# Batch 1's complex product by three real products instead of four, with its sums, and three minima, moved to GpSimd

## The chip, the cores and the metric

One core of a Trainium2 chip runs the whole program. Its engines are TensorE (PE, with PEld for its weight loads), VectorE (DVE), ScalarE (ACT), GpSimd (POOL) and SyncE (SP, which only issues DMAs here). Each engine works through its own queue in order and waits on semaphores for the others. The metric is the device time of one execution in microseconds (us); lower is better.

## The reference, cut to what matters

```python
def _attn_ref(x, w_r, w_i, b_r, b_i):            # x: 8 batches x 3008 x 256
    X = np.fft.rfft(x, axis=1)
    Xr, Xi = X.real, X.imag
    Yr = Xr @ w_r - Xi @ w_i + b_r
    Yi = Xr @ w_i + Xi @ w_r + b_i
    lam = 0.01                                    # soft threshold of both parts
    Yr = np.sign(Yr) * np.maximum(np.abs(Yr) - lam, 0.0)
    Yi = np.sign(Yi) * np.maximum(np.abs(Yi) - lam, 0.0)
    return np.fft.irfft(Yr + 1j * Yi, n=x.shape[1], axis=1)

def _moe_ref(x, w_in, w_out):                     # 24064 x 256, 256 x 2048, 2048 x 256
    h = x @ w_in
    g = np.where(h > 0.0, h, np.exp(np.minimum(h, 0.0)) - 1.0)
    return g @ w_out
```

The output of the first part, its 8 batches one after the other, is the input of the second.

## The kernel before, in words

The second part is the bulk of the work and sets the beat. It runs in steps `i = 0 .. 375`, 47 for a batch (`PER`). A step makes one piece of the hidden layer: `front(i)` multiplies `w_in` by the transposed batch `yT` into two banks of PSUM, `hps` (four matmuls of 512 columns, line 1118; four banks in all, so step i+2 writes the banks of step i); ACT takes the exponential into `Et`; somebody takes the minimum with 1 (`elu`: POOL at line 1169 when the step is "pooled", DVE at line 1171 otherwise; in a step that is "on_act" ACT makes it by another route, lines 1128 and 1133); DVE joins `Et` and `hps` into `gT` (lines 1159 and 1161); and two steps later (`LAG`) `back(i)` multiplies `gT` by `w_out` into `ps_o` (eight matmuls, line 1192). Every eighth step closes a block of 512 rows: DVE and ACT copy `ps_o` to `osb` (line 1203), which SP sends out; the next block writes the same two banks.

Between the steps lies the first part, for the batch after. It is cut into units, and `plan(b)` writes down by hand which unit of batch b+1 goes into which step while batch b's hidden layer runs:

- A, X: the forward transform. A puts its result through DRAM into `Z`. X unit u makes an eighth of the spectrum `XT` from Z and has ACT copy it out of PSUM. In batch 1 units 2g and 2g+1 together use up quarter g of Z; a quarter is 8 neighbours out of every 32 columns of XT.
- M: the complex product, twelve groups of 128 frequencies, two for each of six `Y` tiles. DVE adds the bias into `yb`, POOL clips (`clip`) and subtracts, which is the soft threshold, and `turn_Y` sends the finished Y tile by DMA to `Yx`.
- B, Y: the inverse transform. B unit v needs `Yx` v; its result goes through DRAM to `Bs`, from which Y units make `yT`.

In the order of the code a step's units `f0` come first, then `front(i)`, then DVE's `gT` of step i-1, then the step's `f1` (stores, loads, `turn_Y`), then the minimum of step i, then `back(i-2)`. That is the order on each engine's queue.

Batch 0's first part runs before step 0. While batch 0's hidden layer runs (`plan(0)`), batch 1 gets: X units 0 to 7 in steps 10 to 17, M groups 0 to 5 in steps 18 to 23, B unit 0 in step 24, M groups 6 and 7 in 25 and 26, B 1 in 27, M in 28 and 29, B 2 in 30, M in 31 and 32, B 3 to 5 in 33 to 35, and A units of batch 2 from step 36. The x of batch 2 is loaded on POOL's queue in steps 12, 15 and 18, behind a `gate` in step 12 that waits for Z. A step with an M group is on_act; in plan(0) the other steps from 10 on have their minimum on DVE unless they are free of units.

There are two ways of the complex product. Batches 0 and 1 (`m_group`, line 292) use four products, each of 512 columns with real and imaginary outputs side by side: Xr by (w_r, w_i) and Xi by (-w_i, w_r). From batch 2 on (`unit_M` below its first branch, line 334) there are three of 256 columns: k1 = (Xr + Xi) w_r, then Xi by -(w_r + w_i) and Xr by (w_i - w_r), which with k1 give the two parts. Each is two matmuls, over the halves (`dt`) of the 256 channels. For that POOL adds Xr + Xi (`sum_XT` into the six chunks of `XS` and `busy`, line 260); `three_weights` replaces the weights and one bias by their differences on POOL (lines 276 and 279) in steps 47 to 50; DVE makes two additions from PSUM (lines 340 and 341); POOL adds a bias (line 346), clips (349) and subtracts (350). `XS` lies where `M3` was, of which a copy, `M3x`, is sent in step 6. In PSUM the M groups of batch 1 now share one pair of banks per Y tile ("psF", as the X and B units have it); the later batches have two single banks, `ps` and `k1` ("psM").

Of the kernel before, what the change touches and what calls it, by code (L numbers as in the profile page):

```python
# [24 lines left out]
NS = 32  # L25
# [4 lines left out]
def kernel(  # L30
# [224 lines left out]
    def sum_XT(b, dt, chunks=range(3)):  # L255

        XT = XT_of[b]
        for ch in chunks:
# [3 lines left out]
            )  # L262

    def sum_of(dt, ch):

        if 3 * dt + ch == 5:
            return busy[:]
        if not XS_of:
            XS_of.append(sump.tile([P, 5, 512], BF16, name="XS", tag="XS"))
        return XS_of[0][:, 3 * dt + ch]  # L270

    def three_weights(c, dt):
# [4 lines left out]
        if c == dt == 0:  # L277
            b_r_, b_i_ = (bias_bc[:, D * k : D * k + D] for k in range(2))
            nc.gpsimd.tensor_tensor(b_i_, b_i_, b_r_, ALU.subtract)

    mps_of = {}

# [26 lines left out]
    def unit_M(b, q, i):  # L309
        if b == 1:  # L310
            if i == 0:
                mps_of[q] = unit_ps("mps", False)
            yb, clip = m_group(b, q, i, mps_of[q][:, i, :])
            nc.gpsimd.tensor_scalar(clip[:], yb, LAM, -LAM, ALU.min, ALU.max)
            nc.gpsimd.tensor_tensor(Y_of[b, q][:, i, :], yb, clip[:], ALU.subtract)
            return
        XT, o = XT_of[b], (2 * q + i) * P
# [11 lines left out]
        ]  # L329
        if o == 0 and b > 3:  # L330
            todo.append(todo.pop(0))
# [17 lines left out]
        nc.gpsimd.tensor_scalar(clip[:], yb[:], LAM, -LAM, ALU.min, ALU.max)  # L349
        nc.gpsimd.tensor_tensor(Y_of[b, q][:, i, :], yb[:], clip[:], ALU.subtract)  # L350

# [870 lines left out]
    def plan(b):  # L1222
# [38 lines left out]
        for t, u in enumerate(seq, lead):  # L1261
# [19 lines left out]
            else:  # L1281
                f0[t].append(put(u[0], n1, *u[1:]))
            if u[0] == "M" and u[2] == 1:
                f1[t].append((turn_Y, (n1, u[1])))
            if u == ("B", 5):
# [18 lines left out]
        if n2 < B:  # L1304
            for ci in range(3):
                f1[xs[ci]].append((load_x, (n2, ci)))
        if b and n1 < B:
            f0[seq.index(("X", 4))].append((sum_XT, (n1, 0)))
            f0[seq.index(("X", 7))].append((sum_XT, (n1, 1, range(2 if b < 3 else 3))))
            if b < 3:  # L1310
                f0[seq.index(("M", 2, 0))].insert(0, (sum_XT, (n1, 1, (2,))))
# [5 lines left out]
    for i in range(n + LAG):  # L1317
# [6 lines left out]
        elif i < n:  # L1324
# [12 lines left out]
            else:  # L1337
                on_act = any(f is unit_M for f, a in f0[r])
                pooled = free or i < FILL
            third = calm and bare % 3 == (2 if i // PER == B - 1 else 1)  # L1340
            h = front(i, third, on_act)
        finish_elu()
        if i < n:
# [5 lines left out]
            elu(i, *h, pooled, on_act)  # L1349
            if PER <= i < PER + 4:  # L1350
                three_weights(*divmod(i - PER, 2))
            if 1 <= i < 5:
# [41 lines left out]
```

## Time and profile before

| | us |
|---|---|
| median of 3 runs (lowest, highest) | 871.36 (871.35, 871.52) |
| the profiled execution | 871.1 |
| its span, first to last instruction | 869.3 |
| PE busy | 860.8 |
| ACT busy | 715.4 |
| DVE busy | 666.2 |
| POOL busy | 592.8 |

Busy times are sums over the whole span; matmuls are pipelined, so PE's contains overlaps. In a line of the timeline stand the start, the time from the first start to the last end of the instructions merged in it, the engine, the line of the kernel, the operation, what it writes and reads, the shape, how many instructions (x), and in brackets how long the engine had been idle and who ended that. In a line of groups stand the count (x), the busy time in us, the mean of one in ns and the idle time before.

### The profile page before, as it was taken

The numbers are of one execution on the slowest core, as the hardware profiler recorded it, in microseconds if no ns is written. First come the engines' busy times: TensorE is split into PE (matmuls) and PEld (weight loads), VectorE is DVE, ScalarE is ACT, GpSimd is POOL, SyncE is SP. The second block draws the span as 40 slices with busy tenths as digits, with TensorE's granted clock in tenths as the row PEclk, the third lists the DMA queues.
The fourth block names the chain that finished last, engine by engine and source line by source line (L and its number), as shares of the span: only waits on it lengthen the run. The fifth ranks groups of instructions, "written<-read, shape, count | busy, mean of one in ns | idle before, by whom it ended". The sixth has DMA issues, their size and how long they took to land.

```text
span 869.3 us, 18553 instructions
## 1 busy us (share of the span) xinstructions
PE 860.8 (99%) x6773; PEld 675.8 (78%) x6773; DVE 666.2 (77%) x1103; ACT 715.4 (82%) x1255; POOL 592.8 (68%) x866
## 2 busy tenths in 40 slices
PE   8999999999999999999999999999999999999997
PEld 6567677887788877887778877787877888787776
DVE  8889779697676886778866787677777687788775
ACT  8878888888978889798887988879887888876664
POOL 8671651898657986588846987459874697734664
PEclk9999999999999999999999999999999999999999
DMA  8897446532575135653365432753337313250111
GB/s 248 282 288 213 117 131 193 164 117 73 141 224 170 51 79 168 191 170 92 89 183 172 128 104 78 217 165 107 94 96 213 90 39 85 79 141 25 40 36 49
DMA packets 113597, 116.11 MB, mean 134 GB/s; under 512 B 11569, under 2 KB 103473, under 8 KB 110145
## 3 DMA queue, kind: packets, MB, share of 16 engines
q1 hardware_dynamic: 108512, 86.74, 35.2%
q0 software_dynamic: 4704, 27.92, 9.8%
q8 instruction: 53, 0.87, 0.4%
q14 instruction: 40, 0.32, 0.1%
q10 hardware_dynamic: 288, 0.26, 0.1%
HBM read 53.28 MB, written 48.23 MB: 117 GB/s over the span
## 4 chain that ended last, share of the span: by engine, by line
PE 94%; POOL 2%; DVE 1%; DMA 1%; ACT 1%; issue 0%; DVEq 0%; POOLq 0%
PE ps_o L1192 39%; PE hps L1118 34%; PE mps L334 5%; PE xps L242 3%; PE mps L1118 2%; PE yps L615 2%; PE bps L451 2%; PE mps L292 2%; PE aps L194 2%; POOL Y L350 1%; DMA xt<-in_x_dram 1%; PE aps L186 0%; POOL yb L346 0%; POOL clip L349 0%; DVE gT L1159 0%
## 5 line engine op out<-in xcount | busy, mean ns | idle before, releaser
L1159 DVE SCALAR_TENSOR_TENSOR gT<-Et,hps 128x512 fp32r<-128x512 f32 x630 | 403.1, 682 | 137.0 <-POOL Et L1169 127.0
L1192 PE MATMUL ps_o<-w_out_r,gT 128*128 128x256 f32 x3008 | 477.2, 301 | 0.0
L1192 PEld LDWEIGHTS ps_o<-w_out_r,gT 128*128 128x128 f32 x3008 | 404.4, 189 | 48.0 <-DVE osb L1203 0.2
L1169 POOL TENSOR_SCALAR Et<-Et 128x512 f32<-128x512 f32 x482 | 287.3, 615 | 203.1 <-ACT Et L1130 201.6
L1118 PE MATMUL hps<-yT,w_in_s 128*128 128x512 bf16 (+7 forms) x1620 | 366.7, 353 | 0.3
L1130 ACT ACTIVATE Et<-hps 128x512 f32<-128x512 f32 x514 | 282.7, 610 | 41.7 <-PE hps L1118 38.6
L1118 PEld LDWEIGHTS <-w_in_s 128*128 128x128 bf16 x1728 | 144.1, 98 | 104.7 <-issue 13.1
L1128 ACT ACTIVATE Et<-hps 128x512 f32<-128x512 f32 x192 | 104.5, 597 | 42.0 <-PE hps L1118 41.6
L1133 ACT ACTIVATE Et<-Et 128x512 f32<-128x512 f32 x192 | 110.5, 632 | 0.0
L350 POOL TENSOR_TENSOR Y<-yb,clip 128x512 bf16<-128x512 f32 x72 | 92.7, 1287 | 6.0
L346 POOL TENSOR_TENSOR yb<-yb,bias_bc 128x256 f32<-128x256 f32 x72 | 53.2, 738 | 11.3 <-DVE yb L341 11.2
L150 ACT CAST XT<-xps 128x768 bf16<-128x768 f32 x57 | 45.8, 804 | 14.1 <-PE xps L242 13.9
L341 DVE TENSOR_TENSOR yb<-mps,yb 128x512 f32<-128x512 f32 x72 | 49.8, 692 | 7.2
L150 ACT CAST yT<-yps 128x752 bf16<-128x752 f32 x56 | 44.1, 787 | 13.7 <-PE yps L615 13.5
L1161 DVE SCALAR_TENSOR_TENSOR gT<-hps,Et 128x512 fp32r<-128x512 f32 x78 | 50.2, 686 | 3.3
L349 POOL TENSOR_SCALAR clip<-yb 128x512 f32<-128x512 f32 x72 | 44.1, 613 | 6.3
L150 ACT CAST A<-aps 128x1024 bf16<-128x1024 f32 x40 | 40.7, 1018 | 8.1 <-PE aps L194 5.0
L150 ACT CAST Bz<-bps 128x1024 bf16<-128x1024 f32 x41 | 41.6, 1014 | 5.3 <-PE bps L451 5.0
L340 DVE TENSOR_TENSOR yb<-mps,bias_bc 128x256 f32<-128x256 f32 x72 | 30.5, 424 | 17.5 <-PE mps L334 15.7
L334 PE MATMUL mps<-wcat_s,XT 128*128 128x256 bf16 x288 | 43.2, 273 | 0.0
L1203 DVE COPY osb<-ps_o 128x512 f32<-128x512 f32 x46 | 31.7, 690 | 5.4 <-PE ps_o L1192 3.4
L260 POOL TENSOR_TENSOR XS<-XT 128x512 bf16<-128x512 bf16 x30 | 34.1, 1157 | 2.4 <-ACT XT L150 1.4
(216 smaller groups left out, 673.3 us busy)
## 6 DMA issues: line engine op xcount, KB each, us to landing
xt<-in_x_dram POOLq DMA_DIRECT2D x21, 1024.0 KB, 5.3
out_dram<-osb SPq DMA_DIRECT2D x154, 128.0 KB
Bs<-DB SPq DMA_DIRECT2D x30, 384.0 KB
Yx<-Y SPq DMA_DIRECT2D x166, 64.0 KB
DA<-A SPq DMA_DIRECT2D x19, 512.0 KB
DB<-Bz SPq DMA_DIRECT2D x19, 512.0 KB
Z<-DA SPq DMA_DIRECT2D x21, 384.0 KB
xt<-in_x_dram POOLq DMA_DIRECT2D x6, 512.0 KB, 6.2
```

The source lines that it names most:

```text
L150: nc.scalar.copy(dst, src)
L334: nc.tensor.matmul(out_, lhsT=lhs[:, dt] if lhs is not None else sum_of(dt, ch)[:, oc : oc + P], rhs=w[:, dt, :], start=(dt == 0), stop=(d ...
L346: nc.gpsimd.tensor_tensor(yb[:, D : 2 * D], yb[:, D : 2 * D], bias_bc[:, D : 2 * D], ALU.add)
L350: nc.gpsimd.tensor_tensor(Y_of[b, q][:, i, :], yb[:], clip[:], ALU.subtract)
L1118: nc.tensor.matmul(hps[s][:, c0:c1], lhsT=w_in_s[:, dt, ft * P : ft * P + P], rhs=yT_of[b][:, dt, t0 : t0 + c1 - c0], start=(dt == 0), sto ...
L1128: nc.scalar.activation(Et[:, s], hps[s], AF.Relu, scale=-1.0)
L1130: nc.scalar.activation(Et[:, s], hps[s], AF.Exp)
L1133: nc.scalar.activation(Et[:, s], Et[:, s], AF.Exp, scale=-1.0)
L1159: nc.vector.scalar_tensor_tensor(o, e, -1.0, h, ALU.add, ALU.max)
L1161: nc.vector.scalar_tensor_tensor(o, h, 0.0, e, ALU.max, ALU.add)
L1169: nc.gpsimd.tensor_scalar(e, e, 1.0, 0.0, ALU.min, ALU.max)
L1192: nc.tensor.matmul(po[q][:, j, :], lhsT=gT[:, s, i_ * P : i_ * P + P], rhs=w_out_r[:, ft, :], start=(ft == 0 and j == 0), stop=(ft == NFT ...
```

## The change

Batch 1's M groups take the second way, three products. Its sums are not made by `sum_XT` but by a new `sum_part`, once for each quarter of Z, behind the X units 1, 3, 5 and 7 (steps 11, 13, 15 and 17): three additions on POOL over rows of 8 neighbours, for chunks 0 to 2, 3 to 4 and 5. As in the batches above 3, the product with the sum comes last in batch 1's very first group. `three_weights` moves from steps 47 to 50 to steps 10 to 13. The last subtraction of the batch, of group 11 in step 32, goes from POOL to DVE (`finish_Y`), behind DVE's `gT` of step 31 and ahead of the DMAs of that Y tile. In the steps of B units 0, 1 and 2 of plan(0) (24, 27 and 30) the minimum is POOL's instead of DVE's.

```diff
+    def sum_part(b, g):
+        XT, k = XT_of[b], slice(8 * g, 8 * g + 8)
+        def by_m(v):
+            return v.rearrange("p (m s) -> p m s", s=NS)[:, :, k]
+        sum_of(0, 0)
+        XS, m = XS_of[0][:], 2 * 512
+        for out_, dt, m0, m1 in (
+            (XS[:, 0:3].rearrange("p c n -> p (c n)"), 0, 0, 3 * 512),
+            (XS[:, 3:5].rearrange("p c n -> p (c n)"), 1, 0, m),
+            (busy[:], 1, m, 3 * 512),
+        ):
+            nc.gpsimd.tensor_tensor(
+                by_m(out_), by_m(XT[:, dt, 0, m0:m1]), by_m(XT[:, dt, 1, m0:m1]), ALU.add
+            )
...
     def unit_M(b, q, i):
-        if b == 1:
-            if i == 0:
-                mps_of[q] = unit_ps("mps", False)
-            yb, clip = m_group(b, q, i, mps_of[q][:, i, :])
-            nc.gpsimd.tensor_scalar(clip[:], yb, LAM, -LAM, ALU.min, ALU.max)
-            nc.gpsimd.tensor_tensor(Y_of[b, q][:, i, :], yb, clip[:], ALU.subtract)
-            return
...
-        if o == 0 and b > 3:
+        if o == 0 and (b == 1 or b > 3):
             todo.append(todo.pop(0))
...
-        nc.gpsimd.tensor_tensor(Y_of[b, q][:, i, :], yb[:], clip[:], ALU.subtract)
+        if (b, q, i) == (1, 5, 1):
+            late_Y.append((Y_of[b, q][:, i, :], yb, clip))
+        else:
+            nc.gpsimd.tensor_tensor(Y_of[b, q][:, i, :], yb[:], clip[:], ALU.subtract)
+
+    late_Y = []
+
+    def finish_Y():
+        Y, yb, clip = late_Y.pop()
+        nc.vector.tensor_tensor(Y, yb[:], clip[:], ALU.subtract)
...
             if u[0] == "M" and u[2] == 1:
+                if (b, u[1]) == (0, 5):
+                    f1[t].append((finish_Y, ()))
                 f1[t].append((turn_Y, (n1, u[1])))
...
-        if b and n1 < B:
+        if b == 0:
+            for g in range(4):
+                f0[lead + 2 * g + 1].append((sum_part, (n1, g)))
+        elif n1 < B:
...
-                pooled = free or i < FILL
+                pooled = free or i < FILL or any(f is unit_B and a[1] < 3 for f, a in f0[r])
...
-            if PER <= i < PER + 4:
-                three_weights(*divmod(i - PER, 2))
+            if FILL <= i < FILL + 4:
+                three_weights(*divmod(i - FILL, 2))
```

More of the change, by code (lines that the diff above doesn't have):

```diff
@@ L279, in three_weights @@
             nc.gpsimd.tensor_tensor(b_i_, b_i_, b_r_, ALU.subtract)
-    mps_of = {}
     def m_group(b, q, i, ps, biased=False):
```

## The prediction

> **What bounds the kernel now.** I read the page first, its shares of busy time and its chain of waits:
>
> ```profile
> span 869.3 us, 18553 instructions
> PE 860.8 (99%) x6773; PEld 675.8 (78%) x6773; DVE 666.2 (77%) x1103; ACT 715.4 (82%) x1255; POOL 592.8 (68%) x866
> ...
> PE 94%; POOL 2%; DVE 1%; DMA 1%; ACT 1%; issue 0%; DVEq 0%; POOLq 0%
> ```
>
> TensorE (PE) carries 94% of the chain. Time taken off its instruction stream is time gained, as long as no other engine becomes late at that place. The timeline then shows one M step of batch 1 (steps 18 to 32; four products of 512 columns, line 292) and one of batch 2, which already has the form that batch 1 is to get (six of 256, line 334):
>
> ```profile
> 86.31 0.61 PE L292 MATMUL mps<-wcat_r,XT 128*128 128x512 bf16 x2
> ...
> 87.18 1.03 PE L1118 MATMUL hps<-yT,w_in_s 128*128 128x512 bf16 x4
> ...
> 88.97 0.61 PE L292 MATMUL mps<-wcat_r,XT 128*128 128x512 bf16 x2
> ...
> 179.33 0.39 PE L334 MATMUL mps<-wcat_r,XS 128*128 128x256 bf16 x2
> ...
> 179.76 0.42 DVE L340 TENSOR_TENSOR yb<-mps,bias_bc 128x256 f32<-128x256 f32 x1
> ...
> 180.00 1.03 PE L1118 MATMUL hps<-yT,w_in_s 128*128 128x512 bf16 x4
> ...
> 180.29 0.69 DVE L341 TENSOR_TENSOR yb<-mps,yb 128x512 f32<-128x512 f32 x1
> ...
> 180.90 1.27 DVE L1159 SCALAR_TENSOR_TENSOR gT<-Et,hps 128x512 fp32r<-128x512 f32 x2
> ...
> 181.79 0.39 PE L334 MATMUL mps<-wcat_r,XS 128*128 128x256 bf16 x2
> ```
>
> PE goes from one M group to the hidden layer in 0.87 us with four products, in 0.67 us with six, and from one M step to the next in 2.66 and 2.46 us. So the change is worth 12 x 0.20 = 2.4 us on PE, 0.28% of the time. That is also the most it can give. 0.2% (1.7 us) is about what a measurement of this kernel can tell from no change.
>
> **What GpSimd (POOL) must do for it.** The first row here is the batch's first M group today; the others are batch 2's, where POOL has the work that batch 1 is to get:
>
> ```profile
> 85.68 0.61 POOL L314 TENSOR_SCALAR clip<-yb 128x512 f32<-128x512 f32 x1 [13.28 <-DVE yb L302]
> ...
> 176.86 0.39 PE L334 MATMUL mps<-wcat_r,XS 128*128 128x256 bf16 x2
> ...
> 178.59 0.75 POOL L346 TENSOR_TENSOR yb<-yb,bias_bc 128x256 f32<-128x256 f32 x1 [0.39 <-DVE yb L341]
> ...
> 181.36 0.74 POOL L346 TENSOR_TENSOR yb<-yb,bias_bc 128x256 f32<-128x256 f32 x1
> ...
> 182.18 0.61 POOL L349 TENSOR_SCALAR clip<-yb 128x512 f32<-128x512 f32 x1
> ...
> 182.88 1.29 POOL L350 TENSOR_TENSOR Y<-yb,clip 128x512 bf16<-128x512 f32 x1
> ...
> 184.13 0.74 POOL L346 TENSOR_TENSOR yb<-yb,bias_bc 128x256 f32<-128x256 f32 x1
> ```
>
> Before batch 1's M groups POOL sat idle for 13.28 us. With the new form it needs 184.13 - 181.36 = 2.77 us for each M group, and PE brings one every 2.46. Batch 2 has at most four M groups in a row; batch 1 has six (steps 18 to 23) ahead of its first B step. There POOL falls behind by 0.31 us a group, and the change puts one more thing into its queue at that very place, the minimum of B steps 0 to 2.
>
> **The sums.** For each quarter of Z: 384, 256 and 128 elements.
>
> ```profile
> L260 POOL TENSOR_TENSOR XS<-XT 128x512 bf16<-128x512 bf16 x30 | 34.1, 1157 | 2.4 <-ACT XT L150 1.4 <-DVE XT L148 1.0
> ...
> L971 POOL TENSOR_SCALAR w_in_s<-w_in_f 128x256 bf16<-128x256 f32 x4 | 4.7, 1170 | 0.3
> ...
> L276 POOL TENSOR_TENSOR wcat_s<-wcat_r,wcat_s 128x256 bf16<-128x256 bf16 x2 | 1.3, 672 | 0.0
> ```
>
> Lines 260 and 276 (512 and 256 elements in 1157 and 672 ns) give 1.9 ns an element and 0.19 us an instruction: 0.92 + 0.67 + 0.43 = 2.0 us a quarter, if rows of eight neighbours, 64 bytes apart, run like whole rows. That is the low end. The high end is line 971, which reads single elements 16 bytes apart: (1170 - 190) / 256 = 3.8 ns, so 3.5 us a quarter. I take the low end, since within a row of eight the step is that of line 260. The Trainium skill (GPSIMD Engine Reference, Performance pitfalls for Q7 kernels) has it that reads with a step above 8 bytes cost about half as much again, 2.9 cycles an element for 1.9; line 971 pays far more than that here. By that rule the sums, with an inner step of 2 bytes, cost nothing extra, and if it held for their outer step, 2.8 us a quarter as an estimate, still less than the time of two X steps.
>
> Two X steps are 4.3 us (81.48 to 83.62 below is one), so three quarters hide behind the X units. Two things may delay the first quarter, and both have room: XS takes the place of M3, which SP is still sending at 70 us, and a store to one quarter of XT could be held up by a read of another. The second does not happen: DVE starts on one quarter of batch 0's XT at 21.46 while ACT is on its neighbour until 21.91.
>
> ```profile
> 21.11 0.80 ACT L150 CAST XT<-xps 128x768 bf16<-128x768 f32 x1 [0.77 <-PE xps L242]
> ...
> 21.46 2.00 DVE L148 CAST XT<-xps 128x768 bf16<-128x768 f32 x2 [0.55 <-PE xps L242]
> ...
> 65.18 4.89 SPq L429 DMA_DIRECT2D M3x<-M  x4
> ...
> 81.48 0.51 PE L242 MATMUL xps<-M,Z 128*128 128x96 bf16 x8
> ...
> 82.03 0.80 ACT L150 CAST XT<-xps 128x768 bf16<-128x768 f32 x1 [0.36 <-PE xps L242]
> ...
> 83.62 0.60 PE L292 MATMUL mps<-wcat_r,XT 128*128 128x512 bf16 x2
> ...
> 84.30 0.68 DVE L1171 TENSOR_SCALAR Et<-Et 128x1024 f32<-128x1024 f32 x1
> ...
> 87.59 0.59 POOL L121 DMA_DIRECT2D xt<-in_x_dram  x1
> ```
>
> The fourth quarter does not hide. Its XT is there at 82.83, so its first two sums end at 82.9 + 0.92 + 0.67 = 84.5. PE starts the group at 83.62 and, even with the sum's product put last, wants the second of them at 83.62 + 5 x 0.11 = 84.17 (six products in 0.67 us): **0.35 us lost** on PE. DVE is no earlier (minimum of step 17, 84.30 to 84.98). Its first addition comes 0.43 us after the start of a sum's two products, the second 0.53 after the first and takes 0.69: 84.4 + 0.43 + 0.53 + 0.69 = 86.1, and with the handovers POOL starts on the group at 86.3.
>
> Of what else moves: the gate and two loads of batch 2's x now stand on POOL's queue behind sums, some 4 to 8 us later; their first reader is step 36, eighteen steps on, so nothing. The three weights (4 x 0.67 us and a bias) go from steps 47 to 50 to steps 10 to 13, where POOL is idle; their old place gains nothing, for POOL still waited 0.39 us for DVE at 178.59, ahead of batch 2's M groups.
>
> **Steps 18 to 28.** POOL starts at 86.3, has six groups and the third x load (0.6 us, line 121, queued behind the first group): 86.3 + 6 x 2.77 + 0.6 = 103.5. Only then comes the minimum of B step 0. This is what such lateness does in batch 2 today:
>
> ```profile
> 194.24 1.03 PE L1118 MATMUL hps<-yT,w_in_s 128*128 128x512 bf16 x4
> ...
> 197.47 2.35 POOL L1169 TENSOR_SCALAR Et<-Et 128x512 f32<-128x512 f32 x4
> ...
> 198.12 2.48 DVE L1159 SCALAR_TENSOR_TENSOR gT<-Et,hps 128x512 fp32r<-128x512 f32 x4 [1.65 <-POOL Et L1169]
> 198.19 0.33 PEld L451 LDWEIGHTS <-M3x 128*128 128x128 bf16 x4
> ...
> 198.87 1.19 PE L1118 MATMUL hps<-yT,w_in_s 128*128 128x512 bf16 x4
> ```
>
> POOL reaches the step's Et 3.2 us after that step's hidden layer began, DVE waits 1.65 us, and PE, which writes the hidden layer two steps later into the same banks, starts at 198.87 instead of 198.52 (198.19 and 0.33 of weights) and runs 0.16 us longer: 0.5 us lost. In the changed kernel PE's B step 0 starts at 83.6 + 0.35 + 6 x 2.46 = 98.7, its hidden layer four products or 0.44 us later, at 99.2; POOL comes 4.3 us after that, not 3.2, above all because it starts 2.7 us after PE's first group and not 1.7 (83.62 to 86.3; in batch 2 from 176.86 to 178.59). The two halves of Et are ready at 104.1 and 104.7 (0.59 us each), gT at 104.8 and 105.5. PE wants the banks at 98.7 + 2.26 + 2.46 + 0.67 = 104.1 (2.26 us for a B step, rows below): 0.9 us lost, and 0.15 for the second half. Behind that wait DVE holds step 25's copy of ps_o (line 1203, 512 columns as line 341's 0.69 us), without which PE cannot start the next block: 0.35. Then come M group 7's additions and the next gT: 0.3. Together **1.7 us lost**.
>
> ```profile
> 107.28 0.61 PE L451 MATMUL bps<-Yx,M3x 128*128 128x256 bf16 x4
> ...
> 109.54 0.55 PEld L292 LDWEIGHTS <-XT 128*128 128x128 bf16 x4
> ```
>
> From there POOL recovers: two M groups and a B step are 2 x 2.77 + 1.2 = 6.7 us for it and 2 x 2.46 + 2.26 = 7.2 for PE, so B steps 1 and 2 cost nothing. DVE has 0.42 + 0.69 + 1.27 = 2.4 us in an M step of 2.46, just enough; without the minimum of the B steps (0.69, now POOL's) it catches up there.
>
> **The end of the batch.** The last subtraction is given to DVE, which waits for POOL's clip. The last group starts on PE at about 119.6 and POOL is some 0.4 us behind, so the clip ends near 123.0 and the subtraction (0.69, as line 341) at 123.7. Behind it on DVE stand gT of step 32 and a copy of ps_o: 0.2 us lost. Y is then as late as before, while PE is 0.4 us earlier:
>
> ```profile
> 122.46 1.28 POOL L315 TENSOR_TENSOR Y<-yb,clip 128x512 bf16<-128x512 f32 x1
> ...
> 124.04 1.29 POOL L429 DMA_DIRECT2D Yx<-Y  x2 [0.30 <-POOL Y L315]
> ...
> 127.04 0.61 PE L451 MATMUL bps<-Yx,M3x 128*128 128x256 bf16 x4
> ```
>
> Today Y ends at 123.74 and B step 5 starts, unhindered, at 127.04, 3.3 us later. In the changed kernel it has 3.0: between 0 and 0.3 us lost, and I take 0.
>
> **The sum.** -2.4 + 0.35 + 1.7 + 0.2 = -0.15 us by these steps. Each of the eight waits in it holds a handover between engines that I rounded up by some 0.03 us; I take 0.25 off for that and forecast -0.4. The profiled execution took 871.1 us, 869.3 of it span; the median of the runs shown is 871.36, 0.26 above it. -0.4 from the median: **871.0 us**. Its own range, with the handovers taken all short or all long: 870.3 to 871.8.
>
> **Rivals.** (1) POOL's lateness does not reach PE: only the 0.35 us at the first group are lost, 871.36 - 2.4 + 0.35 = 869.3 us. For it: batch 2 loses just 0.5 us to the same cause. Against it: POOL is 1.1 us later here than in batch 2, and of that only 0.6 comes back, because PE takes 4.9 us from one hidden layer to the next but one, and 4.3 there (194.24 to 198.52).
>
> (2) The sums run at line 971's rate, and the kernel is slower. Four quarters of 3.5 us, the gate and two loads then keep POOL busy without a break from about 71.5 or 73 (when M3 has gone) to beyond 86; the sums that PE's first M group needs end at 86 to 87.5 instead of 84.5, and PE and POOL both start the six groups that much later: +1.5 to +3.0 us on the forecast, 872.5 to 874.0. It decides from about 3 ns an element. For it: the high end of the rows. Against it: the step within a row.
>
> (3) The handover at the end goes wrong: DVE, held by the late clip, is late for steps 33 to 35 and Yx for B step 5, 0.3 + 0.6 us more: 871.9.
>
> That the change doesn't do what it says on PE is not a case: batch 2's rows are the same code.
>
> **How the numbers follow.** Forecast 0.55, rival 1 0.20, rival 2 0.15, rival 3 0.10. Faster by over 0.2% (below 869.6): rival 1, 0.20. Slower by over 0.2% (above 873.1): two thirds of rival 2, and what I have not seen, 0.18. Between: 0.62. The range reaches to rival 1 and to the near end of rival 2: 869.2 to 872.9.
>
> **What would show it.** Right: M steps of 2.46 us in the window of batch 1; a short PE wait for the sums at the first group; POOL without a gap from there to B step 0, DVE waiting for POOL's Et of that step, PE late by about a microsecond two steps after it. Wrong: PE without a gap there (rival 1), single sums of 384 elements well over 1 us (rival 2), PE waiting for Yx (rival 3).

## The result, and the profile after

The changed kernel is slower: 875.10 us median against 871.51 for the kernel before on the same chip, a ratio of 1.0037 (95% interval 1.0024 to 1.0049). The prediction said 871.0, and at most 872.9. The profiled execution took 875.79 us, 874.0 of it span. From its page, the line of busy times and the chain of waits:

```profile
PE 861.9 (99%) x6797; PEld 677.9 (78%) x6797; DVE 671.9 (77%) x1113; ACT 716.1 (82%) x1255; POOL 614.6 (70%) x895
...
PE 87%; POOL 5%; DVE 3%; ACT 2%; DMA 1%; issue 1%; SPq 0%; DVEq 0%; POOLq 0%
```

PE had 94% of the chain before; POOL now has 5% where it had 2, and DVE 3% where it had 1. The first X matmul of step 10 and the first A matmul of step 36 bracket all that the change touches. Here they are in the timeline, first of the kernel before, then of the changed one:

```profile
66.46 0.50 PE L242 MATMUL xps<-M,Z 128*128 128x96 bf16 x8 [0.17 <-DVE yT L148]
...
129.30 0.63 PE L194 MATMUL aps<-xt,M 128*128 128x512 f32 x2
```
```profile
68.09 0.50 PE L242 MATMUL xps<-M,Z 128*128 128x96 bf16 x8 [0.17 <-DVE yT L148]
...
95.07 0.39 PE L343 MATMUL mps<-wcat_r,XS 128*128 128x256 bf16 x2
97.55 0.39 PE L343 MATMUL mps<-wcat_r,XS 128*128 128x256 bf16 x2
...
133.85 0.62 PE L194 MATMUL aps<-xt,M 128*128 128x512 f32 x2
```

The window is 62.84 us before and 65.76 after, 2.9 longer, while the M steps are shorter as foretold (97.55 - 95.07 = 2.48 us). So 5.3 us are lost in it. (The 1.6 us by which the second trace is late at step 10 arise in the start-up; among the profiles of this study that part moves by up to 4 us.) To see where, I took the start of each step's eight matmuls into `ps_o` in both traces, set the difference between them to zero at step 10, and added back the 0.2 us saved in every M step passed. What is left is loss: **2.40 us** by step 25, **1.66** from step 25 to 27 (two steps behind B step 0, which is step 24), 0.01 from 27 to 33, **1.20** from 33 to 36.

**The first 2.40 us.** All runs of line 1171 in the kernel before, and of the same line, now 1189, after (nanoseconds: least, median, most); then the timelines of DVE and POOL in the changed kernel's X steps:

```profile
L1171 DVE TENSOR_SCALAR Et<-Et x39: 682/693/696, 68.9 to 788.2; 128x1024 f32<-128x1024 f32 x39
```
```profile
L1189 DVE TENSOR_SCALAR Et<-Et x36: 681/694/1651, 70.5 to 792.9; 128x1024 f32<-128x1024 f32 x36
```
```profile
79.08 1.38 DVE L1189 TENSOR_SCALAR Et<-Et 128x1024 f32<-128x1024 f32 x1
80.56 1.29 DVE L1179 SCALAR_TENSOR_TENSOR gT<-hps,Et 128x512 fp32r<-128x512 f32 x2
81.77 1.65 DVE L1189 TENSOR_SCALAR Et<-Et 128x1024 f32<-128x1024 f32 x1
83.52 1.29 DVE L1179 SCALAR_TENSOR_TENSOR gT<-hps,Et 128x512 fp32r<-128x512 f32 x2
84.72 1.62 DVE L1189 TENSOR_SCALAR Et<-Et 128x1024 f32<-128x1024 f32 x1
```
```profile
74.08 1.99 POOL L278 TENSOR_TENSOR XS<-XT 128x384 bf16<-128x384 bf16 x2 [4.70 <-DMA M3x<-M]
...
78.92 2.05 POOL L278 TENSOR_TENSOR XS<-XT 128x384 bf16<-128x384 bf16 x2
...
81.32 0.66 POOL L294 TENSOR_TENSOR wcat_s<-wcat_r,wcat_s 128x256 bf16<-128x256 bf16 x1
81.95 1.98 POOL L278 TENSOR_TENSOR XS<-XT 128x384 bf16<-128x384 bf16 x2
...
84.27 0.57 POOL L121 DMA_DIRECT2D xt<-in_x_dram  x1
84.86 2.00 POOL L278 TENSOR_TENSOR XS<-XT 128x384 bf16<-128x384 bf16 x2
```

A minimum that always took 0.69 us takes 1.38 to 1.65 in three of these steps, while POOL adds. It ends 1.54, 1.47 and 1.48 us after POOL's pair of sums began (80.46 - 78.92, 83.42 - 81.95, 86.34 - 84.86): that is the pair's first sum, 0.9 us, and then its own 0.69, within 0.12. The first came 0.16 us after the sum had begun. The second and third came while another instruction was in progress on POOL (a weight difference, a DMA issue), and the sum queued behind it went first as well. In return the pair takes 2.0 us; undisturbed it takes 1.53 (below). `gT`, which reads `hps` from PSUM and `Et` from SBUF, stays at 1.29. With 0.69 + 1.29 = 1.98 us of work in an X step of 2.15, DVE has 0.17 to spare; 0.69 + 0.96 + 0.93 us too much make `gT` late. PE waits for that and, at the second M group, for DVE's additions:

```profile
84.26 1.19 PE L1136 MATMUL hps<-yT,w_in_s 128*128 128x512 bf16 x4 [0.50 <-DVE gT L1179]
...
90.05 0.61 PE L343 MATMUL mps<-wcat_s,XT 128*128 128x256 bf16 x4 [0.23 <-DVE yb L350]
```

From 79.1 us to the second M group the chain of waits holds DVE's instructions alone. PE's weight load did wait for the last quarter's sums, 0.26 us at 86.91 where 0.35 was foretold, but beside this longer wait.

The Trainium skill (SBUF — State Buffer, Who interferes with whom) states this: VectorE and GpSimd share a pair of SBUF ports, `tensor_scalar` from SBUF to SBUF can take both pairs, and whoever comes first blocks the other for a whole instruction, while an operation with one SBUF input outside those modes doesn't. The rows agree with all but one point: two of the three minima waited for more than the instruction in progress.

**The next 1.66 us** are the prediction's B step 0. In the timeline PE waits for `gT`, for whose Et POOL comes late:

```profile
107.36 1.19 POOL L1187 TENSOR_SCALAR Et<-Et 128x512 f32<-128x512 f32 x2
108.00 1.28 DVE L1177 SCALAR_TENSOR_TENSOR gT<-Et,hps 128x512 fp32r<-128x512 f32 x2 [1.51 <-POOL Et L1187]
108.75 1.19 PE L1136 MATMUL hps<-yT,w_in_s 128*128 128x512 bf16 x4 [0.66 <-DVE gT L1177]
```

**The last 1.20 us.** The timeline of the end, and two rows of the DMA view for the 3.5 us from 127.81 on; then the same row of the kernel before, for the 3.5 us from its issue:

```profile
126.17 0.61 POOL L358 TENSOR_SCALAR clip<-yb 128x512 f32<-128x512 f32 x1
126.82 0.69 DVE L368 TENSOR_TENSOR Y<-yb,clip 128x512 bf16<-128x512 f32 x1 [0.65 <-POOL clip L358]
127.81 1.29 POOL L447 DMA_DIRECT2D Yx<-Y  x2 [1.02 <-DVE Y L368]
131.43 0.80 PE L469 MATMUL bps<-Yx,M3x 128*128 128x256 bf16 x4 [0.86 <-DMA Yx<-Y]
```
```profile
q8 instruction: 1, 0.02, 1.6%
...
Yx<-Y POOLq DMA_DIRECT2D x2, 64.0 KB, 3.4
```
```profile
Yx<-Y POOLq DMA_DIRECT2D x2, 64.0 KB, 2.5
```

Y is ready 4.2 us after PE began the last group (123.33 to 127.51), 4.1 foretold, but Yx takes 3.4 us to land; in the kernel before it took 2.5. Among its packets stands an instruction load, a piece of 16 KB of the program itself, on queue 8 (below: the code load). It came 1.43 us after POOL's issue and was one packet of 0.88 us. In the kernel before the nearest one came 6.3 us after the issue.

### The profile page after: what moved, and what is told of

It is laid out like the page before. It is cut to its first block, busy times and chain, and to the rows that moved or that the text cites. A ratio compares the mean times of both kernels' runs of the same rounds, so it can differ in the third digit from the quotient of the medians.

```text
span 874.0 us, 18641 instructions
## 1 busy us (share of the span) xinstructions
PE 861.9 (99%) x6797; PEld 677.9 (78%) x6797; DVE 671.9 (77%) x1113; ACT 716.1 (82%) x1255; POOL 614.6 (70%) x895
## 4 chain that ended last, share of the span: by engine, by line
PE 87%; POOL 5%; DVE 3%; ACT 2%; DMA 1%; issue 1%; SPq 0%; DVEq 0%; POOLq 0%
PE ps_o L1210 37%; PE hps L1136 32%; PE mps L343 5%; PE xps L242 2%; PE mps L1136 2%; PE yps L633 2%; POOL Y L362 2%; PE bps L469 2%; PE aps L194 2%; POOL yb L355 1%; POOL clip L358 1%; DMA Yx<-Y 1%; DVE gT L1177 1%; DVE Et L1189 1%; DVE gT L1179 1%
## 5 line engine op out<-in xcount | busy, mean ns | idle before, releaser
L1187 POOL TENSOR_SCALAR Et<-Et 128x512 f32<-128x512 f32 x488 | 291.7, 617 | 205.9 <-ACT Et L1148 204.4
L1146 ACT ACTIVATE Et<-hps 128x512 f32<-128x512 f32 x192 | 104.8, 597 | 42.1 <-PE hps L1136 41.8
L362 POOL TENSOR_TENSOR Y<-yb,clip 128x512 bf16<-128x512 f32 x83 | 106.9, 1288 | 6.9
L355 POOL TENSOR_TENSOR yb<-yb,bias_bc 128x256 f32<-128x256 f32 x84 | 62.1, 739 | 14.6 <-DVE yb L350 14.5
L350 DVE TENSOR_TENSOR yb<-mps,yb 128x512 f32<-128x512 f32 x84 | 58.1, 692 | 8.4
L358 POOL TENSOR_SCALAR clip<-yb 128x512 f32<-128x512 f32 x84 | 51.7, 615 | 7.4
L349 DVE TENSOR_TENSOR yb<-mps,bias_bc 128x256 f32<-128x256 f32 x84 | 35.6, 424 | 20.3 <-PE mps L343 18.3
L343 PE MATMUL mps<-wcat_s,XT 128*128 128x256 bf16 x336 | 50.5, 273 | 0.2 <-DVE yb L350 0.2
L1179 DVE SCALAR_TENSOR_TENSOR gT<-hps,Et 128x512 fp32r<-128x512 f32 x72 | 46.4, 686 | 3.3
```

The lines of the kernel that those rows point to most:

```text
L343: nc.tensor.matmul(out_, lhsT=lhs[:, dt] if lhs is not None else sum_of(dt, ch)[:, oc : oc + P], rhs=w[:, dt, :], start=(dt == 0), stop=(d ...
L355: nc.gpsimd.tensor_tensor(yb[:, D : 2 * D], yb[:, D : 2 * D], bias_bc[:, D : 2 * D], ALU.add)
L1146: nc.scalar.activation(Et[:, s], hps[s], AF.Relu, scale=-1.0)
L1187: nc.gpsimd.tensor_scalar(e, e, 1.0, 0.0, ALU.min, ALU.max)
```

## The experiments

Losses are in us, from the profiled execution alone, worked out as above (for kernels with four products nothing is added back); the two last columns are the medians, with the kernel before of the same round in brackets, and their ratio over all executions. What PE lost ahead of step 10 has no column: 2.25 us in e3 and 0.82 in e12, e13 and e14.

| kernel | step 10 to 25 | 25 to 27 | 27 to 33 | 33 to 36 | us (before) | ratio, 95% |
|---|---|---|---|---|---|---|
| changed | 2.40 | 1.66 | 0.01 | 1.20 | 875.10 (871.51) | 1.0037 (1.0024 to 1.0049) |
| e1 sums alone; again | 0.01; 0.53 | 0; 0 | 0.01; 0 | -0.01 | 873.08 (871.49); 872.77 (871.48) | 1.0018 (1.0009 to 1.0027) |
| e2 no sums | 1.32 | 1.65 | 0.03 | 1.78 | 874.02 (871.49) | 1.0030 (1.0018 to 1.0042) |
| e3 M3 early | 4.00 | 1.63 | 0.00 | 1.46 | 878.15 (871.49) | 1.0075 (1.0063 to 1.0088) |
| e4 Y on POOL | 2.21 | 1.66 | 0.00 | 1.30 | 875.64 (871.61) | 1.0045 (1.0031 to 1.0059) |
| e5 B minima on DVE | 2.41 | 0.76 | 0.24 | 4.42 | 874.36 (871.61) | 1.0034 (1.0021 to 1.0047) |
| e6 sums on DVE | 5.03 | 1.58 | 0.03 | 1.52 | 876.75 (871.49) | 1.0066 (1.0053 to 1.0078) |
| e7 wide addition | 3.66 | 0.60 | -0.01 | 1.44 | 874.46 (871.61) | 1.0034 (1.0021 to 1.0047) |
| e9 sums on DVE, later | 2.00 | 1.58 | 0.00 | 1.72 | 874.88 (871.61) | 1.0038 (1.0026 to 1.0050) |
| e10 all mended | 2.80 | 1.20 | 1.94 | 1.25 | 876.47 (871.48) | 1.0064 (1.0047 to 1.0081) |
| e11 code shifted | 3.02 | 1.66 | 0.00 | 0.23 | 873.76 (871.48) | 1.0029 (1.0017 to 1.0041) |
| e12 weights earlier | 0.20 | 1.57 | 0.00 | 1.62 | 873.70 (871.35) | 1.0025 (1.0013 to 1.0038) |
| e13 mended, sums on POOL | 1.97 | 0.06 | 0.53 | 0.86 | 872.24 (871.35) | 1.0007 (0.9999 to 1.0016) |
| e14 mended, sums on DVE | 0.30 | 0.06 | 0.53 | 1.15 | 871.84 (871.35) | 1.0003 (0.9994 to 1.0011) |
| e15 the same, spread | 0.92 | 0.06 | 0.43 | 0.29 | 870.14 (871.47) | 0.9985 (0.9977 to 0.9994) |

### The X steps

**e1, and once more:** the kernel before with `sum_part` and its four calls added.

> The kernel before, with the four quarters of sums added on GpSimd in steps 11, 13, 15 and 17, and nobody reading them: batch 1 keeps its four products, so the sums are work done for nothing. The window from the first X matmul of step 10 to the first A matmul of step 36 took 62.84 us before and 65.76 in the changed kernel. Port theory (while GpSimd's sums read and write SBUF, VectorE's 128x1024 minima of the X steps cannot run, and last 1.4 to 1.7 us for 0.69): three or four stretched minima, PE late by 1 to 2 us at the first M groups, window 63.9 to 64.9, time 872.4 to 873.4. Rival theory (the sums are simply late, behind M3's store and each other, and PE waits for them): nobody waits for these, minima at 0.69, window 62.8 to 63.0, time as before.

> The sums alone once more, for one look. Their first profiled execution took 870.99 us, lost nothing (minima of 0.88, 0.88 and 1.02 us, GpSimd's pairs of sums 2.0 instead of 1.6) and was the fastest of 11 runs, whose median is 873.08. If a profile of a run near the median is caught: minima of 1.4 us or more and a window 1 to 2 us longer. If the sums cost nothing in it either, the other runs' time went somewhere else (the start-up).

The first profile lost nothing, the second 0.53 us. Three minima took 0.88, 0.88 and 1.02 us in the first and 1.20, 1.25 and 1.01 in the second. So the sums alone do stretch the minima, and in these two executions DVE made most of it good. Both theories are missed: the port theory's loss of 1 to 2 us, and the rival's minima of 0.69. But the first profile was the fastest of its eleven executions, and their median of 873.08 lies where the port theory put it (872.4 to 873.4). The second's span is 1.7 us longer than that of the kernel before, and 0.9 of it arose in the start-up. What the sums alone cost in a median execution stays open.

**e2:**
```diff
-            for g in range(4):
-                f0[lead + 2 * g + 1].append((sum_part, (n1, g)))
+            f0[lead + 1].append((fill_sums, ()))
...
+    def fill_sums():
+        sum_of(0, 0)
+        nc.gpsimd.memset(XS_of[0][:], 0.0)
+        nc.gpsimd.memset(busy[:], 0.0)
```


> The changed kernel without its sums: XS and its sixth chunk are filled with zeros once, in step 11, so that the products with the sum are of zeros; all else stays. Both theories take the loss at the first M groups away here: no minimum of the X steps above 0.8 us, window 65.76 - 2.4 = 63.3, with 0.3 for what later waits give back 63.3 to 63.8; what is left over the ideal of 62.84 - 2.4 = 60.4 is GpSimd's lateness at B step 0 (1.6) and the end of the batch (1.1). If the window stays above 64.8, the loss at the first groups is not the sums'.

The loss to step 25 falls from 2.40 to 1.32, not to nothing: the first memset that fills the sums (2.23 us on POOL, SBUF written, nothing read) held the minimum beside it to 2.01 us, and the next minimum, beside a DMA issue, took 1.19 (PE lost 1.1 us by step 15 and 0.2 more up to step 25). So the experiment put another such instruction in the place of the sums; it doesn't show a kernel free of them.

**e3:** `-            f1[6].append((turn_M3, ()))` became `+            f1[0].append((turn_M3, ()))`.

> The changed kernel with M3 sent six steps earlier, so that the first quarter's sums do not wait for it (4.7 us in step 11) and do not pile up behind each other. Rival theory (lateness of the sums): the loss at the first M groups goes but for 0.35, window 64.0 or less, time 873.3. Port theory: the sums are made one per two X steps, each meets one minimum (4 stretched, as many as before or one more), but VectorE has an X step between two of them to catch up; 0.7 to 2 us of the loss stays, window 64.5 to 65.8.

The rival falls: the sums no longer waited for M3 and the loss rose to 4.00 us, beyond the port theory's 2 as well. (M3's transfer also held up batch 0's `Bs` on SP's queue; PE waited 2.5 us for it in step 7.) POOL in this kernel, all runs of the minimum, and PE behind the longest one:

```profile
75.91 0.68 POOL L294 TENSOR_TENSOR wcat_s<-wcat_r,wcat_s 128x256 bf16<-128x256 bf16 x1
76.53 1.53 POOL L278 TENSOR_TENSOR XS<-XT 128x384 bf16<-128x384 bf16 x2
78.03 0.41 POOL L278 TENSOR_TENSOR busy<-XT 128x128 bf16<-128x128 bf16 x1
78.41 0.66 POOL L294 TENSOR_TENSOR wcat_s<-wcat_r,wcat_s 128x256 bf16<-128x256 bf16 x1
```
```profile
L1189 DVE TENSOR_SCALAR Et<-Et x36: 682/690/3525, 71.8 to 795.8; 128x1024 f32<-128x1024 f32 x36
```
```profile
80.47 1.57 PE L1136 MATMUL hps<-yT,w_in_s 128*128 128x512 bf16 x4 [1.94 <-DVE gT L1179]
81.48 2.27 PE L1210 MATMUL ps_o<-w_out_r,gT 128*128 128x256 f32 x8
```

One minimum began at 76.09 and ended at 79.61: it waited until POOL's run of weight difference, sums and weight difference, all queued one behind the other, was about over. Here POOL's sums were not stretched at all (1.53). Not all of the 4.00 us is this wait: after PE had stood 1.94 us, its granted clock was 0.50 from about 81.1 to 84.6 us, and eight matmuls into `ps_o` took 2.27 us instead of 1.3. Of the loss 1.4 us fall in that time.

**e6:** `nc.vector` for `nc.gpsimd` in `sum_part`, and `any(f is unit_X or ...)` in `pooled`, so that POOL makes the X steps' minima.

> The changed kernel with the two swapped: VectorE makes the four quarters of sums, GpSimd the minima of the X steps 10 to 17. VectorE has no operation of the kind that it lost time in while GpSimd works (the minima from SBUF to SBUF), except the sums themselves. Port theory: GpSimd's minima (2 x 0.6 us) disturb little, no VectorE row above 1.3 us in the X steps, the first groups lose at most 0.5 instead of 2.4; window 63.3 to 64.0, time 872.9 to 873.6. If what counts is the total of work on the two engines, or the sums' wait for M3, which now holds VectorE: window 65 or more.

The last case of the expectation came: DVE stood 4.56 us waiting for M3's transfer, PE lost 4.7 by step 13, and 0.3 from there to step 25. (As in e3, the granted clock was 0.50 for some 3.5 us after PE's wait of 2.77 us, which is 1.7 us of it at most.) **e9** only moves the first quarter's sums to step 13:

```diff
-                f0[lead + 2 * g + 1].append((sum_part, (n1, g)))
+                f0[lead + 2 * max(g, 1) + 1].append((sum_part, (n1, g)))
```


> The kernel with sums on VectorE and the X steps' minima on GpSimd again, but with the first quarter's sums one place later (step 13, with the second's), so that VectorE does not stand still 4.6 us for M3's transfer. If that stand was the whole of its loss in the X steps (4.7 us, none after it), PE loses at most 0.4 there instead of 2.0 in the changed kernel, and the time is 1.6 to 2.0 us under the changed kernel's, 873.1 to 873.5, with the losses at B step 0 (1.5) and at the end (1.1) as they were. If it is the sums' work or their waits for ACT's XT, loss of over 1 us in steps 13 to 17.

2.0 us where 0.4 was expected. Two quarters in a row, ahead of `gT`, took DVE 3.5 us beside POOL's minima and weight differences: 0.86 us for a sum of 384 elements and 0.62 for one of 128, where the same sums took 0.35 and 0.22 us in e6 with POOL idle. Two SBUF inputs on DVE are enough to collide. By the same section of the Trainium skill a VectorE operation with two SBUF inputs meets a GpSimd instruction that reads SBUF, through the shared read port; these rows agree.

**e12** moves the weights' differences and nothing else:

```diff
-            if FILL <= i < FILL + 4:
-                three_weights(*divmod(i - FILL, 2))
+            if 5 <= i < 9:
+                three_weights(*divmod(i - 5, 2))
```


> The changed kernel with the weights' differences made in steps 5 to 8 instead of 10 to 13; all else stays. The sums alone, with GpSimd otherwise idle between them, cost PE 0 and 0.5 us in their two profiles (minima of 0.9 to 1.0 us), the changed kernel 1.6 to 2.5 (minima of 1.4 to 1.7, one of 3.5 where a weight difference stands between two sums). If a minimum waits until GpSimd's run of queued instructions ends, what counts is how long the runs are: here they are shorter, the X steps lose 0.3 to 1.0, and the time is 873.5 to 874.5. But the sums of the first quarter still wait for M3's transfer and pile up; if that alone makes the runs, or if it is the port as such whatever the runs, the loss stays at 1.6 or more and the time at 875.

All runs of the minimum in e12:

```profile
L1189 DVE TENSOR_SCALAR Et<-Et x36: 681/686/1018, 70.1 to 790.7; 128x1024 f32<-128x1024 f32 x36
```

The loss to step 25 falls from 2.40 to 0.20, its minima take at most 1.02 us, and the median falls by 1.4. (In steps 5 to 8 the differences cost 0.82 us of their own, the pooled minima of steps 6 and 7 coming late behind them.) So in these profiles it was the weights among the sums that made the X steps dear. The expectation's reason, shorter runs of queued instructions, isn't what the rows show: around the minima of 0.88 and 1.02 us POOL went from one instruction to the next within 0.05 us, in e12 as in e1. Over all traces with the sums on POOL the rows sort by what POOL was doing when the minimum came. With a sum in progress (21 times) it waited for no more than the rest of that sum: 0.26 and 0.46 us were left in e12, 0.75 at the first stretched minimum of the changed kernel. With a weight difference in progress and a sum queued behind it (8 times) the sum always went first, for a wait of 0.95 to 1.44 us, and once of 2.84. Without the weights that second case is gone. Why the sum goes first there is not shown.

### B step 0

**e5:** `pooled = free or i < FILL`, as in the kernel before.

> The changed kernel with the minima of B steps 0, 1 and 2 back on VectorE. In the changed kernel GpSimd comes late to B step 0, VectorE's gT waits for it, and PE loses 1.5 us two steps later. Theory of the prediction (GpSimd's lateness reaches PE through that minimum alone): the 1.5 us go, but VectorE, with 2.4 us of work in an M step of 2.46 and 0.69 more in the B steps, gives back 0.3 to 0.8; time 874.0 to 874.5. Rival (GpSimd's lateness reaches PE anyway, through yb and clip buffers and the next M groups): time as the changed kernel, 875 or more.

B step 0 loses 0.76 instead of 1.66: the prediction's theory, with the 0.3 to 0.8 us that DVE was expected to give back. Of the profile's 4.42 us at the end PE stood 2.26 waiting for Yx, which took 4.5 us there, and after that wait the granted clock was again 0.50 for about 3.5 us; this execution was the slowest of its kernel (876.65, median 874.36).

**e7:** in batch 1 DVE's first addition is 512 wide (k1 read twice, both biases), and POOL adds no bias.

> The changed kernel with GpSimd's bias addition taken out of batch 1's M groups: VectorE's first addition is 512 wide (both biases, k1 read twice) instead of 256. GpSimd's work for a group falls from 2.77 to about 2.0 us, under PE's 2.46; VectorE's rises from 2.4 to 2.66, above it. If GpSimd's lateness at B step 0 is what costs 1.5 us there, that goes; if VectorE is the next to be full, each of the six groups in a row costs PE 0.2 us, 1.2 in all, and the time is 874.6 to 875.2; if VectorE's queue absorbs that, 873.5.

B step 0 loses 0.60, but the M steps ahead of it took 2.57 to 2.60 us instead of 2.48, and to step 25 3.66 us are lost instead of 2.40: DVE, with 2.66 us of work expected in each, is the next to be full. The time lies just under the range given for that.

### The end

**e4:** no `finish_Y`; the last subtraction on POOL.

> The changed kernel with the batch's last subtraction back on GpSimd; nothing else. In the changed kernel PE waits 1.1 us for Yx ahead of B step 5, for two reasons that the traces leave mixed: Y ends on VectorE 2.53 us after the group's second addition (2.07 on GpSimd before), and the transfer takes 3.3 to 3.6 us to land (2.4 to 2.5 before). Handover theory (the order on VectorE makes Y late): Y ends 2.1 us after the addition, PE's loss between step 34 and 35 falls by 0.4 to 0.6. Landing theory (what competes with the transfer makes it late): landing stays near 3.4 us, loss falls by at most 0.5 and does not vanish. Time 874.6 to 875.0 either way; if the handover saved as the change has it, 875.5.

Y ended 3.18 us after the addition, not 2.1: POOL was still busy with group 10. So without the move to DVE Y is 0.65 us later, and the end loses 1.30 us instead of 1.20: the last case of the expectation. Yx landed in 2.4 us all the same; the code load now came 0.10 us after the later issue, ahead of the data. The issue itself took 1.64 us instead of 1.29, beside a minimum of DVE's; the Trainium skill (the same section) has it that a VectorE operation can starve GpSimd's writing of descriptors, and this row agrees.

**e11:** `-    for _ in range(18):` became `+    for _ in range(36):`, and `0:256` became `0:128`.

> The changed kernel with its 18 start-up matmuls of 256 columns (on ones, result unused, while PE waits for the first x) made 36 of 128: the same PE time, 36 more instructions in PE's stream ahead of everything. In the changed kernel a 16 KB instruction load (queue 8, one for every 256 PE instructions) goes to a DMA engine 1.4 us after GpSimd issues Yx, and Yx takes 3.4 us to land; in the kernel before it comes 6.3 us after, and Yx takes 2.5; with the subtraction on GpSimd it came 0.1 after, ahead of the data, and Yx took 2.4. Theory (the load delays the one of the 16 DMA engines it goes to): here the load comes some 2.4 us earlier, Yx takes 2.4 to 2.6, and PE's loss ahead of B step 5 falls from 1.1 to 0.1 to 0.3. Rival (the transfer is slow from what else is sent at that moment, DB or the output): 3.3 or more, loss as before. All other losses as in the changed kernel.

The DMA view of the 3.5 us from POOL's issue (130.20) on has no row of queue 8, and of Yx:

```profile
Yx<-Y POOLq DMA_DIRECT2D x2, 64.0 KB, 2.4
```

The code load came 1.68 us ahead of the issue; the end lost 0.23 instead of 1.20, and the median is 1.3 us lower. Over all profiles of this study: in the nine with the code load 1.15 to 2.63 us after the issue Yx took 3.1 to 4.5 us, in the eleven others 2.3 to 2.6. The 2.63 and the 4.5 are e5's, and there the code load came when an undisturbed Yx has landed already; a second instruction load, of 8 KB on queue 14, stood 1.63 us after the issue. How the 4.5 us came about is open.

**e16, e17, e18:** the kernel before with 56 x 82, 48 x 96 and 42 x 110 start-up matmuls.

> The kernel before with its 18 start-up matmuls of 256 columns made 56 of 82: 76 more instructions in PE's stream, which should bring the code load that came 6.3 us after GpSimd's issue of Yx about 5 us earlier, onto the data of Yx. Theory of the code load: it comes 0.9 to 1.7 us after the issue, Yx takes 3.3 to 4.1 us instead of 2.5, and PE, which had 0.6 us to spare there, loses 0.3 to 1.0 ahead of B step 5 in a kernel that has nothing of the change. Otherwise: landing 2.5, nothing lost.

> The kernel before with 48 start-up matmuls of 96 columns. With 56 of 82 (76 more instructions) the code load moved 6.3 us and came 0.04 us after GpSimd's issue of Yx, ahead of the data, and Yx took 2.4 us; with 60 more it should move 4.9 us and come 1.3 to 1.5 us after the issue. Theory of the code load: Yx takes 3.3 to 4.1 us and PE loses 0.3 to 1.3 ahead of B step 5, in the kernel before. Otherwise: 2.5 us, and at most 0.15 lost.

> The kernel before with 42 start-up matmuls of 110 columns, 48 more instructions. 60 and 76 more both moved the code load 6.3 us, to the moment of GpSimd's issue of Yx; 36 more moved it 3.1 us in the changed kernel. If it moves about 4.5 here, it comes 1.8 us after the issue, onto the data: Yx takes 3.1 us or more and PE loses 0.3 to 1.0 ahead of B step 5 (theory of the code load), or 2.5 and nothing (otherwise). If it does not land between 1.1 and 2.7 us after the issue, the run tells nothing.

None put the code load onto the data: it came 0.04 us after, 0.03 ahead of and 3.25 us after the issue; Yx took 2.4, 2.3 and 2.5 us, the end lost 0.08, 0.19 and nothing, and the times are 871.65, 871.60 and 871.76 (ratios 1.0003, 1.0000 and 1.0004, each interval around 1). They agree with the theory but don't test it in a kernel without the change. Nor does the code load move evenly with the count of instructions: 60 and 76 more moved it by the same 6.3 us.

### The losses mended together

**e10:** sums on DVE, two quarters behind `gT`; clip and subtraction of groups 5, 7 and 9 held back behind the B step's minimum; and

```diff
+        late = b == i == 1 and q > 1
+        (nc.vector if late else nc.gpsimd).tensor_tensor(
             yb[:, D : 2 * D], yb[:, D : 2 * D], bias_bc[:, D : 2 * D], ALU.add
         )
```


> Three products with each of the three losses mended: the sums on VectorE and the X steps' minima on GpSimd, with the first two quarters' sums behind gT of steps 11 and 12; GpSimd's clip and subtraction of groups 5, 7 and 9 held back until behind the minimum of the B step that follows, and the small bias addition of groups 5, 7, 9 and 11 on VectorE. Relative to the kernel before, PE gains 2.4 us in the M steps. If the three mechanisms are right: X steps lose at most 0.4 (2.0 in the changed kernel), B step 0 at most 0.4 (1.5), the end 0.3 to 1.3 according to how long Yx takes to land; the time is 870.0 to 871.5. If GpSimd's total work from the first M group to the last is what counts, lateness removed at B step 0 comes back at B steps 1 and 2 and at the end, and the time is 873 or more.

A miss, and a plain one: the four additions of 256 that DVE took over,

```profile
L356 DVE TENSOR_TENSOR yb<-yb,bias_bc x4: 985/1244/1412, 100.5 to 124.8; 128x256 f32<-128x256 f32 x4
```

took 1.24 us in the median, more than on POOL (0.74), with POOL at work beside them. Each made `gT` late: 1.2 us lost behind B step 0 and 1.9 behind the two next. To step 25 it lost 2.80, for the second quarter's sums still met the weights' differences (one of 128 elements took 1.84 us).

**e13** (sums on POOL) and **e14** (on DVE): the weights as in e12, 36 start-up matmuls, group 5 held back behind B step 0's minimum, which alone of the three stays on POOL, and

```diff
-                xs = (12, 15, 18)
+                xs = (12, 14, 16)
```


> Three products, each loss mended with one more or one less instruction on the engine that had room. Sums stay on GpSimd; the weights' differences in steps 5 to 8; loads of x in steps 12, 14 and 16 instead of 12, 15 and 18; of the three moved minima only that of B step 0 stays on GpSimd, ahead of the bias, clip and subtraction of group 5, which are held back behind it; code load shifted as with the 36 start-up matmuls. No addition of GpSimd's is given to VectorE (in the kernel with all mended each took VectorE 1.0 to 1.4 us). From the kernel before: -2.4 in the M steps, X steps +0.3 to 1.0, B step 0 +0.2 to 0.4, B steps 1 and 2 +0.2, end +0.1 to 0.4; time 870.0 to 871.2. If GpSimd's lateness is only pushed on, B step 0 or the end loses over 1 us and the time is over 872.

> As the one before, but the sums on VectorE (the first two quarters' behind gT of steps 11 and 12) and the X steps' minima on GpSimd. With the weights' differences gone from these steps GpSimd has nothing but the minima there, two instructions of 0.6 us a step, and VectorE's sums wait for at most one or two of them: X steps lose 0 to 0.4, time 869.6 to 870.8. If VectorE's sums are held up as in the kernel with all mended (2.0 us), the weights had no part in it, and the time is 872.

Holding group 5 back settles B step 0 (0.06 us). In e13 the X steps lose 1.97 again, with minima of 1.08, 1.87 and 1.61 us: the loads of x now stand between the sums, and the two longest minima came while such a load was being issued, with a sum behind it that went first. In e14, where POOL has nothing but minima and loads, they lose 0.30, as expected of it. Both missed their times, above all since both still pay 0.8 us for the weights in steps 5 to 8 and 0.9 to 1.2 at the end, where DVE, with B step 2's minimum, was late for the last groups.

**e15** is e14 with the weights' differences in steps 7, 8 and 9, the bias's in step 10, and B step 2's minimum on POOL.

> The kernel with the sums on VectorE and the losses mended, with two more moves: the weights' differences spread over steps 7, 8 and 9 and the bias's in step 10, where GpSimd waits 0.3, 0.8 and 2.0 us for ACT (made in steps 5 to 8 they cost PE 0.83 us, the minima of steps 6 and 7 coming late behind them); and the minimum of B step 2 back on GpSimd, which stood idle 1.8 us behind it while VectorE, with that minimum, was 0.6 us late for the two last groups. Expected: nothing lost ahead of step 10, X steps 0.1 to 0.3, B step 0 at most 0.2, the end 0.3 to 0.6 instead of 0.8 with 0.4 ahead of it; together -1.0 to -1.8 us on the kernel before, 869.6 to 870.4. If the end depends on the transfer alone and not on when Y is ready, 870.9.

870.14 us against 871.47, ratio 0.9985 (0.9977 to 0.9994): faster than both kernels, inside the range expected. Of the 0.92 us to step 25, 0.6 are a wait for Z's transfer in step 12 (e18, with nothing of the change, lost 0.4 to the same wait). With it the parts are -2.4 + 0.92 + 0.06 + 0.43 + 0.29 = -0.7, and the spans of the two profiles differ by 0.6; without it they are -1.3, which is the difference of the medians. So the 2.4 us on PE are real, and by the medians a bit over half could be kept.

## Why the prediction was wrong, point by point

- **PE's saving** of 2.4 us: right (M steps of 2.48, and the sums above close with it).
- **The sums.** Their size was right: 1.53 + 0.41 us a quarter where nothing disturbs them, 2.0 predicted. The step that failed is the sentence that three quarters "hide behind the X units". It asked only whether POOL would be done in time, not what DVE does in that time, and in these traces DVE's minima are held up while POOL adds. The price was 0.35 us; it was 2.40. (The wait that the 0.35 stood for came, with 0.26, beside the longer one for DVE.) The Trainium skill's rule that I weighed, on steps of reading, decided nothing; its rule on the shared ports (SBUF — State Buffer, Who interferes with whom) was the one that spoke against the change, and it is missing from the prediction.
- **M3's wait** "had room" for the first quarter's sums, but not for what it did to the rest: started at 74.08, the sums stood back to back with the three weights and the loads, which I had put down as free because POOL was idle there. In e12, without the weights there, 0.20 was lost instead of 2.40; in e3, where M3's wait is gone and the weights stay, more was lost, not less.
- **B step 0**: right in mechanism (e5, e13) and size, 1.66 us for 1.7, though its own times give 0.7 for the first bank (104.8 - 104.1) where it put 0.9; 0.8 came. **B steps 1 and 2**: right, 0.01 for nothing.
- **The end.** The order on DVE cost 0.16 us for the 0.2 predicted, and Y was ready 4.2 us after the last group began for 4.1 predicted. What failed is "between 0 and 0.3 us lost, and I take 0" for Yx, which took the 3.3 us from Y to B step 5 out of one trace: it was 3.9, and 1.0 lost. Rival 3 had that price (0.9), from a late DVE; the cause was the code load (e11).
- **The sum.** 0.35 + 1.7 + 0.2 became 2.40 + 1.66 + 1.20: -0.15 became +2.9 in the trace and +3.6 between the medians; the 0.7 between those two is not traced. Rival 2's times (up to 874.0) come nearest, but by sums at line 971's rate, which did not occur: the chance of slower, 0.18, was far too small because VectorE's side of the sums was not among the cases.

## What to carry to other kernels

An idle engine is not free room: before work goes to GpSimd, look in the trace for what VectorE does beside it from SBUF to SBUF, since each stops the other here, and move other GpSimd work out of the same steps (e12) or leave it the minima alone (e14). Where VectorE must share the time, give it the operations that read PSUM. A transfer's time in one trace is that of its neighbours, and one more or one less instruction far ahead can change the neighbours.

## What the runs showed of the hardware that I had not expected

- Which of the two waits is decided anew at each instruction. With a sum in progress the minima took 0.7 to 1.5 us (POOL's pairs stretched from 1.53 to 2.0); with a weight difference in progress and a sum behind it 1.6 to 2.1, and once 3.52. With a DMA issue in progress, 0.11 us of it left and a sum behind it, both happened: 0.68 us (e1, e4, e13) and 1.61 (e5, e7, e13). Even a memset, which reads nothing, held them (2.01).
- A 256-element addition from SBUF took VectorE 0.99 to 1.41 us beside a busy GpSimd, longer than GpSimd's own 0.74.
- Instruction loads are part of the DMA traffic. There are 53 of 16 KB in the traces of before and after, about one for every 256 of PE's matmuls and weight loads, and those near Yx took 0.9 to 1.5 us each. That Yx, spread over many DMA engines, waits for the one that has this packet is my reading; the traces don't name the engine of a packet.
- A long wait of PE can be followed by a slower clock. Within about a microsecond after PE's waits of 1.94 (e3), 2.26 (e5) and 2.77 us (e6) the granted clock fell to 0.50 for about 3.5 us, 1.7 us of PE's time each. After the waits of 0.8 to 1.6 us in the other traces, in these steps, it stayed at 1.00, and it did so too after one of 2.51 us in e3 (step 7).
